# Part of an attention and MLP kernel's transfers moved from SyncE's queue to GpSimd's, and others held back

## The chip, the cores and the metric

The kernel runs on one core of a Trainium2 chip. The core has five engines that run side by side, each in its own order of instructions: TensorE (PE, with its weight loads shown apart as PEld), VectorE (DVE), ScalarE (ACT), GpSimd (POOL) and SyncE (SP). Data moves by DMA. An engine issues a transfer in its own instruction order (rows "SPq", "ACTq"), and 16 DMA engines carry it out; the issue takes a fraction of a microsecond, the landing several. The metric is the device time of one execution, in microseconds (us), the median of several runs.

## The reference

The kernel computes a gated mix of two branches over one sequence of 2048 tokens of 448 features, in float32. Cut to what matters:

```python
g = sigmoid((x * gate_w).sum(-1, keepdims=True))
q, k, v = split_heads(x @ wqkv)            # 16 heads of 28
idx = pos[:, None] - 2 * arange(8)         # 8 keys, every second position back
logits = einsum("bhsd,bhswd->bhsw", q, k[idx]) * 28 ** -0.5   # masked where idx < 0
a = einsum("bhsw,bhswd->bhsd", softmax(logits), v[idx]) @ wo
r = relu(x @ w1 + b1)                      # 1792 wide
b = (r * r) @ w2 + b2
out = g * a + (1 - g) * b
```

## The kernel before

Every float32 product is made of three matmuls of a shortened type: each operand is split into a high part (a ScalarE copy that rounds) and a low part (VectorE, or at one place GpSimd, subtracts the high part from the raw value), and high x high, high x low and low x high are added up in PSUM. So every weight and every token tile that arrives as a raw load costs ScalarE and VectorE an operation per slice before TensorE can use it. The contraction's last 64 rows are kept twice, so two matmuls of 64 rows run side by side on the two halves of TensorE; "a pair" or "a step" below is such a couple. When an accumulator changes halves, a one-element ScalarE instruction (`turn`, L360; `touch`, L748, in the MLP) orders the two halves. TensorE waits for these small instructions, and they stand in ScalarE's order with everything else.

Tokens come in four chunks of 512, chunk 0 to 3. Stage one makes q, k and v of each chunk (L353, L441): chunk 0 all at once (`qkv_first`), the others in two halves of two 128-token tiles (`qkv_two`). ScalarE evacuates the sums to staging tiles `st` (L375), of which there are three, and SP stores them to DRAM (`q_d`, `k_d`, `v_d`, L390). The last half of chunk 3 is woven with the first MLP matmuls. Then the MLP runs over the chunks in the order 3, 0, 1, 2. Token chunks are brought by `x_load` into one of two raw buffers and by `x_bring` into their split tiles (L727 on ScalarE, L730 on VectorE). Chunk 2 overwrites the tiles of chunk 0, and chunk 3 those of chunk 1, so the split tokens of chunks 0, 1 and 2 are first spilled to DRAM (`x_d`; L884 for chunk 0, `x_spill` L744 for 1 and 2) and reloaded for the MLP. w1 comes in four pieces (`w1_piece`: L675 into `early`, L665 into a raw buffer), the first half of w2 in two (`w2_piece`, L665; high parts L708, low parts L710), the second half row by row later.

Attention is not made on TensorE. It goes over eight units, two halves of the tokens (`par`) times four groups of four heads. For each unit, q and k (L513, L517) and v (L527) are loaded back from DRAM with eight tokens to a partition; GpSimd multiplies (`qk_piece` L551, `av_piece` L563), VectorE reduces (L555, L573), and a small softmax goes over GpSimd (mask L600, subtract the maximum L606, normalise L615), VectorE and ScalarE (exponent L607). The first unit can start when chunk 1's stores have landed. Its results go through DRAM and a transposing load to the output projection on TensorE (accumulators `a`), which is placed between MLP groups once its loads are in.

The order of all this on ScalarE, VectorE, GpSimd and SP is not written by hand. `Plan` is a list scheduler that runs while the program is built: each job has an engine, a cost, dependencies, a priority (TURN first, LAST last) and an earliest time `at`, in nanoseconds of the plan's own clock. A transfer is a job with `move=(packets, size)`; `wire` is the plan's time at which the DMA is free. `LAND` is an extra distance that a job keeps from a transfer it depends on, by the job's priority. When TensorE's order advances, `Plan.step` takes the jobs that can begin. On the chip only the order that results counts, with the semaphores: an engine executes its next instruction as soon as that one's operands are ready, and holds everything behind it until then.

All transfers but three small ones were issued by SP before the change.

Of the kernel before, what the change touches and what calls it, by code (L numbers as in the profile page):

```python
# [45 lines left out]
LAND = (0.0, 0.0, 500.0, 700.0, 2000.0, 2000.0)  # L46
# [10 lines left out]
class Plan:  # L57
# [4 lines left out]
    def __init__(self):  # L62
# [3 lines left out]
        self.port = self.wire = 0.0  # L66
# [29 lines left out]
    def begin(self, j):  # L96
        r = max(j.at, self.free[j.eng])
        for d in j.deps:
            e = self.end(d)
            if e is None:  # L100
                return None
            r = max(r, e + LAT + (LAND[j.prio] if d.eng == SYNC else 0.0))
        if j.prio > NEXT and r < self.hold[j.eng] < r + j.cost:
            r = self.hold[j.eng]
        if j.move and j.prio >= MID:
            r = max(r, self.wire - BACKLOG)
            if self.quiet[0] < r + j.cost < self.quiet[1]:
                r = self.quiet[1]
        if j.move and j.prio > NEXT:
            if r < self.calm < max(r + j.cost + 1250.0, self.wire) + j.move[0] * (8.0 + j.move[1] / 25.2) / 16 - 1250.0:  # L110
                r = self.calm
        return max(r, self.port) if j.port else r

    def step(self, limit):
# [70 lines left out]
def gated_mix_kernel(ctx: ExitStack, tc: tile.TileContext, xT, wqkv, w1, w2, wo, b1, b2, out):  # L185
# [87 lines left out]
    def dma(fn, packets, size, *deps, prio=MID, at=0.0):  # L273
        return add(SYNC, 430.0, fn, *deps, prio=prio, at=at, move=(packets, size))
# [216 lines left out]
    def attention():  # L491
# [130 lines left out]
        load_qk(1, *early_read)  # L622
        load_v(0)
# [21 lines left out]
    def gates(par):  # L645
        e = smp.tile([P, 32], F32, tag="e", name=f"e{par}")[:, :NS]
        a = add(ACT, 195.0, lambda: nc.scalar.activation(e, zt[:, par], AF.Exp, scale=-1.0), *z_jobs[par], prio=MID)
        a = add(ACT, 210.0, lambda: nc.scalar.activation(e, e, AF.Copy, bias=1.0), a, prio=MID)
        a = add(DVE, 200.0, lambda: nc.vector.reciprocal(gt[:, par], e), a, prio=MID)
        a = add(ACT, 195.0, lambda: nc.scalar.activation(g1t[:, par], gt[:, par], AF.Copy, scale=-1.0, bias=1.0), a)  # L650
        gate_jobs[par] = a
# [7 lines left out]
    def raw_load(i, name, src, view, packets, size, *deps, prio=MID, at=0.0):  # L659
# [3 lines left out]
        def load():  # L663
            hold[0] = rawp.tile([P, 4, 512], F32, tag="raw", name=name)
            nc.sync.dma_start(view(hold[0]), src)  # L665
        return hold, dma(load, packets, size, *held, *deps, prio=prio, at=at)
# [716 lines left out]
```

## Time and profile before

| | us |
|---|---|
| median of 3 runs | 392.4 |
| lowest and highest run | 392.34 and 511.83 |
| the profiled execution, its own time | 393.65 |
| its span, first to last instruction | 391.9 |

The granted TensorE clock was 0.998 of full speed. The span holds 9284 instructions and 73.76 MB of transfers. To read the rows: a timeline row has its start in us from the span's start, the duration of the merged instructions, engine, line, operation, output<-input by the program's names, the count (x), and in brackets how long the engine stood idle before it and what ended that. A row of a window has the window, its length, the busy time and count of PE, PEld, DVE, ACT and POOL, the granted clock, the mean busy share of the 16 DMA engines and GB/s. A row of the list of transfers has the size and the median time from issue to landing. In a wait row stand the total, the number of waits and the longest one.

### The profile page before, as it was taken

The numbers are of one execution on the slowest core, as the hardware profiler recorded it, in microseconds if no ns is written. First come the engines' busy times: TensorE is split into PE (matmuls) and PEld (weight loads), VectorE is DVE, ScalarE is ACT, GpSimd is POOL, SyncE is SP. The second block draws the span as 40 slices with busy tenths as digits, with TensorE's granted clock in tenths as the row PEclk, the third lists the DMA queues.
The fourth block names the chain that finished last, engine by engine and source line by source line (L and its number), as shares of the span: only waits on it lengthen the run. The fifth ranks groups of instructions, "written<-read, shape, count | busy, mean of one in ns | idle before, by whom it ended". The sixth has DMA issues, their size and how long they took to land.

```text
span 391.9 us, 9284 instructions
## 1 busy us (share of the span) xinstructions
PE 386.9 (99%) x3828; PEld 370.9 (95%) x3828; DVE 258.8 (66%) x348; ACT 205.8 (53%) x501; POOL 262.4 (67%) x171
## 2 busy tenths in 40 slices
PE   9999999999999999999999999999999999999996
PEld 8999999989999999999999999999999999999995
DVE  4525522477585778778655989779666686668454
ACT  4857866352566576444555545345616344456740
POOL 0000000999999999959999796999998979662000
PEclk9999999999999999999999999999999999999999
DMA  7999998998165062645203689655635220226745
GB/s 239 383 358 320 372 365 306 374 375 294 50 214 189 0 214 84 220 155 177 89 2 135 227 204 282 210 129 137 198 128 163 87 95 2 89 62 160 139 113 190
DMA packets 64955, 73.76 MB, mean 188 GB/s; under 512 B 32592, under 2 KB 57744, under 8 KB 64528
## 3 DMA queue, kind: packets, MB, share of 16 engines
q1 hardware_dynamic: 64480, 72.79, 57.5%
q8 instruction: 30, 0.49, 0.5%
q10 hardware_dynamic: 432, 0.38, 0.3%
q14 instruction: 13, 0.11, 0.1%
HBM read 45.71 MB, written 28.25 MB: 189 GB/s over the span
## 4 chain that ended last, share of the span: by engine, by line
PE 95%; DMA 3%; ACT 1%; SPq 0%; issue 0%; DVE 0%; DVEq 0%
PE b L353 32%; PE h L353 32%; PE qkv L353 19%; PE a L353 7%; DMA w2raw<-w 3%; PE qkv L441 2%; PE warm L819 1%; PE a L1173 1%; ACT w2ah L708 1%; SPq L390 0%; ACT qkv L360 0%; DVE bt_b L1056 0%; DVEq L1378 0%; SPq L665 0%
## 5 line engine op out<-in xcount | busy, mean ns | idle before, releaser
L551 POOL TENSOR_TENSOR pp<-q,k 128x896 f32<-128x896 f32 x56 | 116.6, 2120 | 77.9 <-DMA k<-k_d 66.9
L563 POOL TENSOR_TENSOR pp<-lg,v 128x896 f32<-128x896 f32 x64 | 113.9, 1870 | 9.6 <-DVE o L573 5.3
L353 PE MATMUL h<-x,w1h 64*128 64x512 f32 x672 | 109.9, 376 | 0.0
L353 PE MATMUL qkv<-wqh,x 64*128 64x448 f32 (+1 forms) x528 | 81.9, 350 | 0.7 <-ACT qkv L360 0.7
L555 DVE TENSOR_REDUCE lg<-pp 128x32 f32<-128x896 f32 x64 | 67.2, 1079 | 17.8 <-POOL pp L551 17.8
L805 DVE TENSOR_TENSOR h<-h,h 128x512 fp32r<-128x512 f32 x56 | 38.7, 691 | 50.8 <-ACT h L804 50.6
L353 PEld LDWEIGHTS h<-x,w1h 64*128 64x128 f32 x672 | 64.5, 186 | 7.6 <-DMA x<-x_d 0.3
L573 DVE TENSOR_REDUCE o<-pp 128x112 f32<-128x896 f32 x64 | 67.5, 1066 | 0.4 <-POOL pp L563 0.4
L353 PE MATMUL b<-w2bh,h 64*128 64x448 f32 x448 | 64.3, 349 | 0.0
L353 PE MATMUL b<-w2ah,h 64*128 64x448 f32 x448 | 64.2, 349 | 0.0
L353 PE MATMUL h<-x,w1l 64*128 64x512 f32 x336 | 64.2, 376 | 0.0
L353 PEld LDWEIGHTS qkv<-wqh,x 64*128 64x128 f32 x528 | 56.4, 186 | 1.0 <-ACT qkv L360 1.0
L801 ACT ACTIVATE h<-h,b1z 128x512 f32<-128x512 f32 x56 | 36.7, 655 | 37.0 <-PE h L353 37.0
L353 PE MATMUL qkv<-wql,x 64*128 64x448 f32 (+1 forms) x264 | 52.6, 349 | 0.0
L353 PEld LDWEIGHTS b<-w2ah,h 64*128 64x128 f32 x448 | 43.7, 193 | 0.7
L353 PEld LDWEIGHTS b<-w2bh,h 64*128 64x128 f32 x448 | 43.6, 193 | 0.7
L353 PE MATMUL b<-w2al,h 64*128 64x448 f32 x224 | 39.7, 349 | 0.0
L353 PE MATMUL b<-w2bl,h 64*128 64x448 f32 x224 | 39.7, 349 | 0.0
L353 PEld LDWEIGHTS h<-x,w1l 64*128 64x128 f32 x336 | 32.2, 186 | 3.3
L803 ACT ACTIVATE h<-h 128x512 fp32r<-128x512 f32 x56 | 33.4, 597 | 1.6
L375 ACT ACTIVATE st<-qkv 128x448 f32<-128x448 f32 x48 | 24.7, 540 | 16.6 <-PE qkv L353 9.0
L804 ACT ACTIVATE h<-h 128x512 f32<-128x512 f32 x56 | 33.2, 592 | 0.0
(111 smaller groups left out, 523.5 us busy)
## 6 DMA issues: line engine op xcount, KB each, us to landing
v<-v_d SPq DMA_DIRECT2D x8, 840.0 KB, 6.2
x_d<-x SPq DMA_DIRECT2D x12, 512.0 KB, 8.3
x<-x_d SPq DMA_DIRECT2D x12, 512.0 KB, 3.9
k<-k_d SPq DMA_DIRECT2D x7, 840.0 KB, 7.2
q_d<-st SPq DMA_DIRECT2D x8, 448.0 KB, 7.1
k_d<-st SPq DMA_DIRECT2D x8, 448.0 KB, 7.9
v_d<-st SPq DMA_DIRECT2D x8, 448.0 KB, 7.9
o_d<-o SPq DMA_DIRECT2D x16, 224.0 KB, 2.1
```

Source lines behind the costliest of these rows:

```text
L353: nc.tensor.matmul(woven_out(acc.pt, acc.n), a[rows], woven(w[rows]), start=acc.todo == acc.all, stop=acc.todo == 1)
L375: nc.scalar.activation(st[0][:, :, t % 2].rearrange("p (i g) c -> p i g c", i=2), unwoven(pt[:, :D]).rearrange("p i (g c) -> p i g c", c=C ...
L441: nc.tensor.matmul(woven_out(acc.pt, NQ), a, woven(w), start=k == j == 0, stop=False)
L551: nc.gpsimd.tensor_mul(pr.rearrange("p (w c) -> p w c", w=W), q[:, s:s + 1].to_broadcast([P, W, C]), k[:, s:s + W])
L555: nc.vector.tensor_reduce(lgs[i][:, s], pr.rearrange("p (w h d) -> p w h d", w=W, h=HG), axis=AX.X, op=ALU.add)
L563: nc.gpsimd.tensor_mul(pr.rearrange("p (h d w) -> p w h d", h=HG, w=W), lgs[i][:, s][:, :, :, None].to_broadcast([P, W, HG, DH]), vs[i][:, ...
L573: nc.vector.tensor_reduce(o_t[par, s][:, g * C:(g + 1) * C], pr.rearrange("p (c w) -> p c w", w=W), axis=AX.X, op=ALU.add)
L708: his = [add(ACT, cost_act(D), lambda k=k: nc.scalar.activation(w2ah[:, i0 + k], hold[0][:, k, :D], AF.Copy), got, prio=LATE) for k in ran ...
L801: a = add(ACT, 656.0, lambda pt=pt, r=r: nc.scalar.activation(pt, pt, AF.Relu, bias=b1t[:, f + r:f + r + 1]), ready, *bias_job[:2], prio=NEXT)
L803: b = add(ACT, 600.0, lambda pt=pt, hh=hh: nc.scalar.activation(hh, pt, AF.Square), a, prio=NEXT)
L804: a = add(ACT, 600.0, lambda pt=pt: nc.scalar.activation(pt, pt, AF.Square), b, prio=NEXT)
L805: low = add(DVE, 690.0, lambda pt=pt, hh=hh, hl=hl: nc.vector.tensor_sub(hl, pt, f32(hh)), a, prio=NEXT)
```

## The change

Fifteen transfers are issued by GpSimd instead of SP: the three token loads (chunks 1 to 3), the four w1 pieces, and the eight spills of chunks 0 and 1. The loads of w2's first half get an earliest planned time of 82000, the spill of chunk 2 one of 86000, the first unit's v one of 75000. The second unit's q and k depend on the landing of the first unit's. The gates of both token halves are made at once after chunk 3 instead of once after chunk 1 and once after chunk 3. The low parts of v's weights are made by one subtraction over three slices. The planner gets a wire for each of the two queues, an issue cost of 1000 on GpSimd, and a larger distance (`LAND`) for jobs of priority LATE, which the w1 and w2 copies have.

```diff
-LAND = (0.0, 0.0, 500.0, 700.0, 2000.0, 2000.0)
+W2_LOAD, X_SPILL, V_LOAD = 82000.0, 86000.0, 75000.0
+LAND = (0.0, 0.0, 500.0, 700.0, 4500.0, 2000.0)
...
-            self.free[SYNC] = s + j.cost + 45.0
-            self.wire = max(s + j.cost + 1250.0, self.wire) + packets * (8.0 + size / 25.2) / 16
-            j.done = self.wire + 450.0
+            self.free[j.eng] = s + j.cost + 45.0
+            other = POOL if j.eng == SYNC else SYNC
+            begin = max(s + j.cost + 1250.0, self.wire[j.eng])
+            time = packets * (8.0 + size / 25.2) / 16
+            both = min(time, max(0.0, self.wire[other] - begin) / 2)
+            self.wire[j.eng] = begin + time + both
+            self.wire[other] += both
+            j.done = self.wire[j.eng] + 450.0
...
-    def dma(fn, packets, size, *deps, prio=MID, at=0.0):
-        return add(SYNC, 430.0, fn, *deps, prio=prio, at=at, move=(packets, size))
+    queue = {SYNC: nc.sync, POOL: nc.gpsimd}
+
+    def dma(fn, packets, size, *deps, prio=MID, at=0.0, by=SYNC):
+        return add(by, 430.0 if by == SYNC else 1000.0, fn, *deps, prio=prio, at=at, move=(packets, size))
...
-        load_qk(1, *early_read)
-        load_v(0)
+        load_qk(1, *early_read, got["q", 0], got["k", 0])
+        load_v(0, event(V_LOAD))
...
-    def gates(par):
+    def gates():
...
-    def raw_load(i, name, src, view, packets, size, *deps, prio=MID, at=0.0):
+    def raw_load(i, name, src, view, packets, size, *deps, prio=MID, at=0.0, by=POOL):
...
-            nc.sync.dma_start(view(hold[0]), src)
-        return hold, dma(load, packets, size, *held, *deps, prio=prio, at=at)
+            queue[by].dma_start(view(hold[0]), src)
+        return hold, dma(load, packets, size, *held, *deps, prio=prio, at=at, by=by)
...
-            got = dma(lambda: nc.sync.dma_start(hold[0], w1[i]), 512, 1792, *deps, prio=MID)
+            got = dma(lambda: nc.gpsimd.dma_start(hold[0], w1[i]), 512, 1792, *deps, prio=MID, by=POOL)
...
-        hold, got = raw_load(buf, f"w2raw{i0}", w2[:, i0:i0 + n], lambda r: r[:, :n, :D], 128 * n, 1792, *deps, prio=MID)
+        hold, got = raw_load(buf, f"w2raw{i0}", w2[:, i0:i0 + n], lambda r: r[:, :n, :D], 128 * n, 1792, *deps, prio=MID, by=SYNC,
+                             at=W2_LOAD)
...
-        x_stored[c] = [dma(lambda j=j: nc.sync.dma_start(x_d[c, j], f32(x.t[j])), 128, 4096, *x.parts[j], prio=MID if c < 2 else LATE)
-                       for j in range(4)]
+        by = POOL if c < 2 else SYNC
+        x_stored[c] = [dma(lambda j=j: queue[by].dma_start(x_d[c, j], f32(x.t[j])), 128, 4096, *x.parts[j],
+                           prio=MID if c < 2 else LATE, by=by, at=0.0 if c < 2 else X_SPILL) for j in range(4)]
...
+    def wv_split():
+        n = block(2)
+        his = [add(ACT, cost_act(D), lambda k=k: nc.scalar.activation(wqh[:, k, n], raws[2][:, k], AF.Copy), event(13000.0),
+                   prio=SOON) for k in range(3)]
+        low = add(DVE, cost_dve(3 * D), lambda: nc.vector.tensor_sub(wql[:, :, n], raws[2], f32(wqh[:, :, n])), *his,
+                  prio=SOON, port=True)
+        for k in range(3):
+            wq_jobs[2, k] = (his[k], low)
...
-            gates(par)
+        if c == 3:
+            gates()
```

The order of instructions that the planner makes of it changes at three places that matter below. The first is ScalarE in chunk 3's first half, the place of w2's copies (`w2ah`). Before, they stand after the last evacuations of chunk 2 (`st`) and ahead of the first turns of chunk 3 (L360, accumulators `qkv_0_0` and so on, named by tile and kind: 0 is q, 1 is k, 2 is v):

```order
L375 ACTIVATE st_3_1_1179<-qkv_2_1_1049 128x4x112
L375 ACTIVATE st_2_2_1201<-qkv_3_2_1052 128x4x112
L708 ACTIVATE w2ah<-w2raw_1116 128x448 x4
L708 ACTIVATE w2ah<-w2raw_1155 128x448 x3
L360 ACTIVATE qkv_0_0_1222<-b1z 1x1
L360 ACTIVATE qkv_1_1_1225<-b1z 1x1
L360 ACTIVATE qkv_1_0_1223<-b1z 1x1
```

In the changed kernel (where L360 has become L369, L375 L384, L607 L616 and L708 L718) they stand after the last evacuations of chunk 3's first half, ahead of and between the turns of its second half, with the first unit's exponent (`lg`) among them:

```order
L384 ACTIVATE st_1_1_1360<-qkv_0_1_1225 128x4x112
L384 ACTIVATE st_0_2_1381<-qkv_1_2_1228 128x4x112
L718 ACTIVATE w2ah<-w2raw_1270 128x448 x4
L616 ACTIVATE lg_1015<-lg_1015 128x256
L369 ACTIVATE qkv_2_0_1403<-b1z 1x1
L369 ACTIVATE qkv_3_1_1406<-b1z 1x1
L718 ACTIVATE w2ah<-w2raw_1344 128x448
L369 ACTIVATE qkv_3_0_1404<-b1z 1x1
L369 ACTIVATE qkv_2_2_1407<-b1z 1x1
L718 ACTIVATE w2ah<-w2raw_1344 128x448 x2
```

Seven copies have moved half a chunk later, and the exponent, which stood after those turns, stands ahead of them. The second place is ScalarE at the start of chunk 1, where chunk 2's tokens are brought. Before, the four copies (`x_0` to `x_3` from `xraw`) lie among the turns:

```order
L360 ACTIVATE qkv_0_0_494<-b1z 1x1
L360 ACTIVATE qkv_1_1_497<-b1z 1x1
L727 ACTIVATE x_0_584<-xraw_244 128x512
L360 ACTIVATE qkv_1_0_495<-b1z 1x1
L360 ACTIVATE qkv_0_2_500<-b1z 1x1
L727 ACTIVATE x_1_585<-xraw_244 128x512
L727 ACTIVATE x_2_586<-xraw_244 128x512
L360 ACTIVATE qkv_0_1_496<-b1z 1x1
L360 ACTIVATE qkv_1_2_504<-b1z 1x1
L727 ACTIVATE x_3_587<-xraw_244 128x512
```

In the changed kernel (L727 is L737) all four lie ahead of the first turn:

```order
L737 ACTIVATE x_0_540<-xraw_257 128x512
L737 ACTIVATE x_1_541<-xraw_257 128x512
L737 ACTIVATE x_2_542<-xraw_257 128x512
L737 ACTIVATE x_3_543<-xraw_257 128x512
L369 ACTIVATE qkv_0_0_496<-b1z 1x1
L369 ACTIVATE qkv_1_1_499<-b1z 1x1
L369 ACTIVATE qkv_1_0_497<-b1z 1x1
```

So the turns now stand behind whatever those copies wait for. The third place is SP from the last stores of chunk 1 on. Before, the loads of the first and the second unit (`q`, `k` and `qk`) lie interleaved, and v and w2 follow:

```order
L390 DMA v_d<-st_2_2_842 128x4x224
L513 DMA q_931<-q_d 128x896
L513 DMA qk_939<-q_d 128x896
L517 DMA k_954<-k_d 128x1680
L517 DMA qk_939<-k_d 128x1680
L527 DMA v_976<-v_d 128x1680
L390 DMA q_d<-st_0_0_1001 128x4x224
L390 DMA k_d<-st_1_1_1011 128x4x224
L390 DMA v_d<-st_0_2_1029 128x4x224
L665 DMA w2raw_1116<-w 128x4x448
L665 DMA w2raw_1155<-w 128x3x448
```

In the changed kernel (L390 is L399, L513 L522, L517 L526) the second unit's come after the first unit's and the biases:

```order
L399 DMA v_d<-st_2_2_840 128x4x224
L522 DMA q_896<-q_d 128x896
L526 DMA k_926<-k_d 128x1680
L914 DMA b1z<-b 128x7
L915 DMA b1z<-b 128x7
L916 DMA b2t<-b 16x448 x2
L522 DMA qk_1012<-q_d 128x896
L526 DMA qk_1012<-k_d 128x1680
L399 DMA q_d<-st_0_0_993 128x4x224
```

The first unit's v and w2 now come later in the queue, w2's first load behind chunk 2's last stores, and w2's second behind the third unit's q and k. On GpSimd the moved transfers stand ahead of the first product, so that its order starts, after constants, with these:

```order
L674 DMA xraw_242<-xT 128x2048
L674 DMA xraw_257<-xT 128x2048
L684 DMA early<-w 128x1792
L905 DMA x_d<-x_0_177 128x1024
L905 DMA x_d<-x_1_178 128x1024
L905 DMA x_d<-x_2_179 128x1024
L905 DMA x_d<-x_3_180 128x1024
L684 DMA early<-w 128x1792
L674 DMA w1raw_557<-w 128x4x448
L755 DMA x_d<-x_353 128x1024 x4
L674 DMA xraw_665<-xT 128x2048
L674 DMA w1raw_787<-w 128x4x448
```

Before, none of these stood there; the first product followed the constants.

More of the change, by code (lines that the diff above doesn't have):

```diff
@@ L65, in __init__ @@
         self.jobs = {e: [] for e in self.free}
-        self.port = self.wire = 0.0
+        self.port = 0.0
+        self.wire = {SYNC: 0.0, POOL: 0.0}
         self.count = 0
@@ L101, in begin @@
                 return None
-            r = max(r, e + LAT + (LAND[j.prio] if d.eng == SYNC else 0.0))
+            r = max(r, e + LAT + (LAND[j.prio] if d.eng and d.move else 0.0))
         if j.prio > NEXT and r < self.hold[j.eng] < r + j.cost:
@@ L105, in begin @@
         if j.move and j.prio >= MID:
-            r = max(r, self.wire - BACKLOG)
+            r = max(r, self.wire[j.eng] - BACKLOG)
             if self.quiet[0] < r + j.cost < self.quiet[1]:
@@ L109, in begin @@
         if j.move and j.prio > NEXT:
-            if r < self.calm < max(r + j.cost + 1250.0, self.wire) + j.move[0] * (8.0 + j.move[1] / 25.2) / 16 - 1250.0:
+            if r < self.calm < max(r + j.cost + 1250.0, self.wire[j.eng]) + j.move[0] * (8.0 + j.move[1] / 25.2) / 16 - 1250.0:
                 r = self.calm
@@ L860, in gated_mix_kernel @@
     nc.vector.tensor_sub(x.x8, rx[:, 3], f32(x.x7))
-    plan.t, plan.wire = START, 15000.0
+    plan.t = START
+    plan.wire[SYNC] = 15000.0
     plan.now = 9800.0
```

24 lines of the change are left out of this document (12 added, 12 removed).

## The prediction

> **What bounds the kernel now.** I read the page first (busy shares, then the chain by engine), then TensorE's waits, then the timeline of TensorE at the one wait found there.
>
> ```profile
> PE 386.9 (99%) x3828; PEld 370.9 (95%) x3828; DVE 258.8 (66%) x348; ACT 205.8 (53%) x501; POOL 262.4 (67%) x171
> ...
> PE 95%; DMA 3%; ACT 1%; SPq 0%; issue 0%; DVE 0%; DVEq 0%
> ...
> PE qkv L353 <- ACT qkv L360: 0.7, 1, 0.7
> ...
> 83.24 0.35 PE L353 MATMUL qkv<-w7h,x 64*128 64x448 f32 x1
> 83.29 0.35 PE L353 MATMUL qkv<-wqh,x 64*128 64x448 f32 x1
> 84.31 0.46 PE L353 MATMUL qkv<-wqh,x 64*128 64x448 f32 x2 [0.67 <-ACT qkv L360]
> ```
>
> TensorE is busy in 386.9 of 391.9 us, and between its first matmul and its last one it waits once. Pairs start 0.19 us apart (82.87, 83.06, 83.24 in this stretch), so the next was due at 83.48 and came at 84.31: 0.83 us lost, of which the wait list counts 0.67. The chain's 3% "DMA" is the work behind that wait and not 3% of idle TensorE. Who held the wait, in the timelines of SP and ScalarE, a 10 us window and the list of transfers:
>
> ```profile
> 69.53 3.50 SPq L665 DMA_DIRECT2D w2raw<-w  x2
> ...
> 77.48 0.98 ACT L375 ACTIVATE st<-qkv 128x448 f32<-128x448 f32 x2
> 80.73 3.38 ACT L708 ACTIVATE w2ah<-w2raw 128x448 fp32r<-128x448 f32 x7 [2.27 <-DMA w2raw<-w]
> 84.02 0.61 ACT L360 ACTIVATE qkv<-b1z 1x1 f32<-1x1 f32 x6
> ...
> 70.00:80.00 10.00, 10.00 (x108) 10.00 (x107) 5.43 (x5) 3.63 (x12) 10.00 (x6) 1.00 1.06 376
> ...
> w2raw<-w SPq DMA_DIRECT2D x1, 896.0 KB, 11.2
> ```
>
> ScalarE had nothing else from 78.46 on, stood 2.27 us for w2's first load, which took 11.2 us on a full DMA (share 1.06), then copied seven slices for 3.38 us. The turns (L360), for which TensorE waits, stand behind them.
>
> **The change, part by part.**
> *w2 held back.* In the new order the seven copies leave this place for one half a chunk later; the turns then follow the evacuations that end at 78.46 and are done well before 83.48. Gain: 0.83 us, no more, since TensorE starts its pairs without a gap on both sides. What is late next is the place the copies go to (timelines of GpSimd, ScalarE, TensorE, VectorE):
>
> ```profile
> 68.33 16.52 POOL L551 TENSOR_TENSOR pp<-q,k 128x896 f32<-128x896 f32 x8 [66.89 <-DMA k<-k_d]
> 84.76 9.38 POOL L551 TENSOR_TENSOR pp<-qk 128x896 f32<-128x896 f32 x3
> 94.10 0.65 POOL L600 TENSOR_TENSOR lg<-lg,mask 128x256 f32<-128x256 f32 x1
> ...
> 98.81 0.64 POOL L606 TENSOR_TENSOR lg<-lg,mx 128x256 f32<-128x256 f32 x1
> ...
> 90.36 0.98 ACT L375 ACTIVATE st<-qkv 128x448 f32<-128x448 f32 x2 [0.72 <-PE qkv L353]
> ...
> 99.48 0.42 ACT L607 ACTIVATE lg<-lg 128x256 f32<-128x256 f32 x1 [0.17 <-POOL lg L606]
> ...
> 96.54 0.35 PE L353 MATMUL qkv<-wql,x 64*128 64x450 f32 x2
> ...
> 82.74 3.99 DVE L710 TENSOR_TENSOR w2al<-w2raw,w2ah 128x1792 fp32r<-128x1792 f32 x1 [0.89 <-ACT w2ah L708]
> ```
>
> There ScalarE now has, between the evacuations and the next turns, four w2 copies (3.38/7 = 0.48 each, 1.9 in all) and the first unit's exponent. Less the 0.83, the evacuations end at 90.5 and the copies at 92.4. TensorE first needs those turns where q's second half begins, one step ahead of the row at 96.54: 96.35, now 95.5. Turn pair 0.26 and exponent 0.42 leave 94.8 as the latest end of GpSimd's subtraction (L606). Ahead of that stand 13 products at 16.52/8 = 2.065, the mask 0.65 and the subtraction 0.64: 28.1 us. (Before it took 31.1: three products took 9.38 beside the w2 subtraction of 3.99 on VectorE, which now comes later.) So attention must start by 94.8 - 28.1 = 66.7 instead of 68.33.
>
> *Second unit's loads behind the first's.* The second unit's q (448 KB) no longer stands ahead of the first unit's k on SP:
>
> ```profile
> 59.28 0.33 SPq L513 DMA_DIRECT2D q<-q_d  x1
> 59.66 0.42 SPq L513 DMA_DIRECT2D qk<-q_d  x1
> 60.69 0.32 SPq L517 DMA_DIRECT2D k<-k_d  x1
> ...
> 58.00:60.00 2.00, 2.00 (x26) 2.00 (x24) 0.44 (x2) 1.52 (x6) 0.00 (x0) 1.00 0.76 237
> 60.00:62.00 2.00, 2.00 (x24) 2.00 (x22) 1.69 (x2) 1.88 (x10) 0.00 (x0) 1.00 0.89 299
> 62.00:64.00 2.00, 2.00 (x26) 2.00 (x24) 0.86 (x3) 1.67 (x5) 0.00 (x0) 1.00 0.95 341
> ```
>
> The windows' last two columns are the DMA's busy share and GB/s. 448 KB, 0.459 MB, at 341 GB/s is 1.3 us. With fifteen transfers on a queue of their own, the idle share of 58 to 62 can be filled too: 2 x 0.24 + 2 x 0.11 = 0.7 us. Start then at 68.33 - 2.0 = 66.3, 0.4 ahead of the limit: TensorE loses 0. Ends: no move at all, 68.33, costs 1.6 us of TensorE; the second unit's k (840 KB) out of the way too, 3.9 + 0.7, gives 63.7 and costs 0. I stand nearer the late end, because only one transfer's place is certain. The first values' load (held back) stood behind k already: 0.
>
> [...]
>
> *Fifteen transfers issued by GpSimd.* No row shows a DMA issue on GpSimd. The nearest are SP's issues of the same tiles (spills L744 and L884, token and w1 loads), then chunk 1 on ScalarE and TensorE:
>
> ```profile
> L744 SPq DMA_DIRECT2D x_d<-x x8: 426/704/3340, 34.3 to 83.1; - x8
> ...
> 10.70 0.93 SPq L665 DMA_DIRECT2D xraw<-xT  x2
> ...
> 23.82 3.40 SPq L884 DMA_DIRECT2D x_d<-x  x3
> ...
> DMA to landing us min/median/max: 6.4/7.6/7.6
> ...
> xraw<-xT SPq DMA_DIRECT2D x3, 1024.0 KB, 7.6
> early<-w SPq DMA_DIRECT2D x2, 896.0 KB, 8.8
> ...
> 20.00:30.00 10.00, 10.00 (x108) 10.00 (x108) 1.72 (x3) 5.25 (x16) 0.00 (x0) 1.00 0.99 351
> ...
> 34.22 0.26 ACT L360 ACTIVATE qkv<-b1z 1x1 f32<-1x1 f32 x2 [0.98 <-PE qkv L353]
> ...
> 36.37 0.63 ACT L727 ACTIVATE x<-xraw 128x512 fp32r<-128x512 f32 x1 [0.18 <-DVE x L730]
> ...
> 35.89 0.37 PE L353 MATMUL qkv<-wql,x 64*128 64x450 f32 x2
> ```
>
> Issue: 15 x 0.43 = 6 us to 15 x 3.34 = 50 us of GpSimd, between 10.7 and the 66.3 to which it waits for k anyway: 0 on the path. SP loses fifteen issues, none of which held TensorE: 0. What can cost is the landing. The four copies that bring chunk 2's tokens (L727) now stand ahead of chunk 1's first turns; they overwrite chunk 0's tokens, so they wait for its four spills (L884). TensorE needs the turns one step ahead of the row at 35.89, at 35.7; less a turn pair (0.26) and the last copy (0.63), the fourth spill must land by 34.8. By bytes: two token loads (1024 KB), a w1 piece (896), four spills (512) and SP's four stores beside them (448) are 6.95 MB, 19.8 us at 351 GB/s; from a first issue at 10.7 + 1 that is 31.5, 3.3 early, and TensorE loses 0. Other end: were each GpSimd transfer to land before the next moves, 11.7 + 2 x 7.6 + 8.8 + 4 x 7.6 = 66.1, a stall of 31.3. The first is nearer: SP issued three spills in 3.40 us though each took 7.6 to land, so transfers overlap.
>
> *The rest.* w2's second load (672 KB) stands on SP behind the third unit's q and k, which wait for the first unit's products, 66.3 + 16.5 = 82.8. With the issues it goes out at about 84 and, taking the 11.2 of the first again, lands by 95.2; its first copy is due ahead of the second turns, needed nine steps (1.7 us) after the first ones' 95.5: 95.2 + 0.48 + 0.26 = 95.9 of 97.2, so 0. Behind the same wait on SP stand the third spill, which nothing in this stretch reads, and the stores of chunk 3's first half, whose evacuations end only at 90.5: 0.
>
> ```profile
> 13.94 1.70 DVE L270 TENSOR_TENSOR wql<-wqraw,wqh 128x448 fp32r<-128x448 f32 x3 [0.98 <-ACT wqh L267]
> ...
> 60.30 1.56 DVE L682 TENSOR_TENSOR w1l<-w1raw,w1h 128x1344 fp32r<-128x1344 f32 x1 [1.86 <-ACT w1h L680]
> ...
> 23.22 0.35 PE L353 MATMUL qkv<-w7h,x 64*128 64x448 f32 x2
> ...
> 58.48 0.21 ACT L650 ACTIVATE zg<-zg 128x8 f32<-128x8 f32 x1 [1.02 <-DVE zg L649]
> ```
>
> V's low parts in one subtraction take 1.56 instead of 1.70; started after the third copy (14.8) they are there at 16.4, and the V matmuls begin nine steps ahead of the row at 23.22, at 21.5: 0. The gates at once drop one set of four small operations, which ended at 58.7 with nobody waiting: 0. TensorE's matmuls are the same 3828; a block of 42 of the output projection moves one group later: 0.
>
> Sum: the profiled execution took 393.65 (span 391.9 and 1.75 around it); less 0.83 it is 392.8. The median of the runs, 392.4, lies 1.25 below it; the same step gives **391.6**.
>
> **Rivals.**
> 1. *No room on the wire.* The bytes taken out of k's way are all: start 67.0, the exponent holds the turns 0.3 us, 391.9. For it: the shares near 1. Against: 0.76 and 0.89 just where k waits. [...]
> 2. *Attention hardly starts earlier*, since k also waits for its own stores. Each microsecond past 66.7 costs one; at 68.33 it is 393.2, slower than before. It decides against the change from a start of 67.5, where the 0.83 is used up. For it: SP issued k at 60.69, 1.0 after the second unit's q, so a wait stood between. Against: FIFO order on SP takes the 448 KB out.
> 3. *GpSimd's queue is slow* and the spills land late ahead of chunk 1's turns. Past 34.8 it costs one for one: break-even at 35.6, over 2% (8 us) past 43.4, and 423 at the serial end; at 37 to 38 it is 393.8 to 394.8. For it: no row shows this queue. Against: 3.3 us of room.
> 4. *The wait only moves*: w2's second load lands after 96.5 and holds the second turns; two microseconds late is 393.6. For it: 11.2 for the first on a full DMA. Against: it is smaller, and 1.57 MB of w2 have left the stretch ahead.
>
> **How the numbers follow.** Forecast 0.60, rival 1 0.14, rival 2 0.10, rival 3 0.11 (0.04 of it past 2%), rival 4 0.05. The forecast's own spread is about half a microsecond, that of its term: 391.0 to 392.1. From 391.0 to 394.0 lie the forecast, rivals 1, 2 and 4 and the mildest of 3. Two per cent is 7.8 us, about what a measurement of this kernel can tell from no change: faster by that 0.01 (the only wait is 0.83), slower 0.04, within it 0.95.
>
> **What would show it.** Right: no wait for L360 on TensorE, w2's copies after 90, first product at 65.5 to 66.7, GpSimd's last transfer issued before 55. Wrong: a TensorE wait near 35 (rival 3), or near 95 behind the exponent (1, 2) or behind a w2 copy (4).

## The result, and the profile after

The changed kernel takes 404.51 us (median of 6 runs, 402.85 to 406.16) against 392.44 before; the ratio is 1.0296 with an interval of 1.0276 to 1.0316. It is 3% slower where 391.6 (391.0 to 394.0) was forecast. The profiled execution took 403.14, span 401.3, against 393.65 and 391.9. So the two profiles differ by 9.5 us and the medians by 12.1: the profile of before lies 1.2 above its median and that of the change 1.4 below. The granted clock was 0.996 in the three faster runs of the change and 0.992 to 0.994 in the three slower ones; no trace shows what those three waited for.

First the page and the waits of TensorE after the change:

```profile
PE 390.3 (97%) x3828; PEld 371.5 (93%) x3828; DVE 260.6 (65%) x345; ACT 204.6 (51%) x498; POOL 270.8 (67%) x186
...
PE qkv L362 <- ACT qkv L369: 5.2, 2, 3.3
PE qkv L362 <- ACT st L384: 1.2, 2, 0.8
```

The one wait of before (0.7 behind w2's copies) is gone. In its place stand four others, 6.4 us together (and one of 0.3 for a reload near 310 us). The timeline of TensorE says where they are, and the windows (busy us and instructions of TensorE, of its weight loads, VectorE, ScalarE, GpSimd, then granted clock, DMA share, GB/s) what happened around them:

```profile
30.04 0.46 PE L362 MATMUL qkv<-wqh,x 64*128 64x448 f32 x2 [3.35 <-ACT qkv L369]
36.33 0.45 PE L362 MATMUL qkv<-wqh,x 64*128 64x448 f32 x1 [0.75 <-ACT st L384]
41.05 0.45 PE L362 MATMUL qkv<-wqh,x 64*128 64x448 f32 x1 [0.46 <-ACT st L384]
45.45 0.46 PE L362 MATMUL qkv<-wqh,x 64*128 64x448 f32 x2 [1.87 <-ACT qkv L369]
...
30.00:32.00 2.00, 1.96 (x14) 1.83 (x16) 0.00 (x0) 0.17 (x2) 0.54 (x1) 0.63 1.04 397
32.00:34.00 2.00, 2.00 (x14) 1.83 (x12) 0.00 (x0) 0.00 (x0) 0.54 (x1) 0.51 1.04 398
34.00:36.00 2.00, 1.58 (x17) 1.23 (x13) 0.00 (x0) 0.27 (x1) 0.45 (x1) 1.00 1.04 389
```

All of it lies between 26 and 46 us, in the chunks 0 and 1, far from the place that the change was meant for. After the wait of 3.35 us the granted clock was 0.63 and 0.51, and TensorE got 14 matmuls into 2 us where the undisturbed kernel gets 108 into 10; from 34 on it was 1.00 again.

The start of TensorE's n-th matmul, compared between two traces, turns this into a sum. The table gives for each execution how much later (+) or earlier it started the n-th matmul than the profiled execution of before:

| matmul | start before | changed kernel | fifteen on SP | all but the queue | w2 alone | before, second profile |
|---|---|---|---|---|---|---|
| 150 | 21.52 | +0.47 | +0.01 | +0.16 | -0.12 | -0.14 |
| 300 | 35.70 | +9.75 | +0.44 | +0.16 | -0.12 | -0.14 |
| 750 | 78.33 | +9.85 | +0.55 | +0.16 | -0.12 | -0.14 |
| 900 | 93.51 | +8.88 | -0.43 | -0.82 | -1.10 | -0.60 |
| 1200 | 123.57 | +8.89 | -0.42 | -0.63 | -0.66 | +0.67 |
| 3000 | 304.08 | +8.71 | -0.60 | -0.81 | -0.62 | +0.50 |
| 3150 | 319.30 | +9.45 | -0.23 | -0.16 | +0.03 | +0.49 |
| last | 388.02 | +9.45 | -0.23 | +0.02 | +0.21 | +0.50 |

(The other columns are experiments told below.) In the changed kernel 0.46 is there from the first microseconds; the four gaps add 3.52, 1.09, 0.79 and 2.06; the stretch at the low clock adds 1.8. That is 9.7 of the 9.85 that stand at matmul 750. Between matmuls 750 and 900 it then gains 0.97, the w2 wait that was removed, and between 3000 and 3150 it loses 0.74 to a wait for the reload of the last tokens.

Who held the four waits, in the timelines of ScalarE, SP and GpSimd, and SP's stores from issue to landing between 14 and 33 us:

```profile
21.17 0.52 ACT L384 ACTIVATE st<-qkv 128x448 f32<-128x448 f32 x1
28.45 1.42 ACT L384 ACTIVATE st<-qkv 128x448 f32<-128x448 f32 x3 [6.77 <-DMA q_d<-st]
...
35.73 0.54 ACT L384 ACTIVATE st<-qkv 128x448 f32<-128x448 f32 x1 [5.57 <-DMA q_d<-st]
...
40.45 0.54 ACT L384 ACTIVATE st<-qkv 128x448 f32<-128x448 f32 x1 [2.81 <-DMA k_d<-st]
...
16.74 1.61 SPq L399 DMA_DIRECT2D q_d<-st  x2
29.46 0.91 SPq L399 DMA_DIRECT2D k_d<-st  x2
...
10.53 1.27 POOL L674 DMA_DIRECT2D xraw<-xT  x2 [9.08 <-DMA wqraw<-wqkv]
11.78 0.53 POOL L684 DMA_DIRECT2D early<-w  x1
12.30 2.12 POOL L905 DMA_DIRECT2D x_d<-x  x4
18.03 0.55 POOL L684 DMA_DIRECT2D early<-w  x1 [3.60 <-DMA xraw<-xT]
27.18 0.77 POOL L674 DMA_DIRECT2D w1raw<-w  x1 [8.61 <-issue]
...
DMA to landing us min/median/max: 10.9/12.3/17.6
```

Read it from the end. ScalarE copies two finished blocks of q, k or v into a staging tile, and SP stores the tile; there are three. The fourth tile to be filled needs the first store to have landed. Before, these stores landed in 5.5 to 6.3 us (same view of the kernel before, 14 to 33 us: 5.5/6.1/6.3), so the tile was free in time. Now SP issues the first two from 16.74 on, much as it did (16.28 before), but they take 11.6 and 17.6. ScalarE stands 6.77 us at 28.45, and behind it in its order stand the turns (L369) for which TensorE waits. GpSimd, with nothing else to do and no wait on those transfers, had issued seven of them by 14.42 (two token loads, a w1 piece and four spills, 4992 KB or 5.1 MB); before, SP issued only the two token loads ahead of the q stores, and the spills after the k stores, at 23.82.

The list of queues from 22 to 26 us shows how the two then share the DMA:

```profile
DMA packets 714, 1.64 MB, mean 409 GB/s; under 512 B 39, under 2 KB 396, under 8 KB 714
...
q0 software_dynamic: 357, 1.32, 80.7%
q1 hardware_dynamic: 357, 0.32, 22.9%
```

q0 is GpSimd's queue, q1 SP's; the columns are packets, MB and share of the 16 engines' time. 357 against 357 packets: in these 4 us each queue got as many packets as the other, and since SP's stores move 896 bytes in one and GpSimd's mostly 4096 (its spills), the stores got a fifth of the bytes (0.32 of 1.64 MB). How the next packet is chosen the trace doesn't show.

### The profile page after: what moved, and what is told of

It is laid out like the page before. It is cut to its first block, busy times and chain, and to the rows that moved or that the text cites. A ratio compares the mean times of both kernels' runs of the same rounds, so it can differ in the third digit from the quotient of the medians.

```text
span 401.3 us, 9297 instructions
## 1 busy us (share of the span) xinstructions
PE 390.3 (97%) x3828; PEld 371.5 (93%) x3828; DVE 260.6 (65%) x345; ACT 204.6 (51%) x498; POOL 270.8 (67%) x186
## 3 DMA queue, kind: packets, MB, share of 16 engines
q0 software_dynamic: 2256, 11.01, 7.2%
## 4 chain that ended last, share of the span: by engine, by line
PE 86%; DMA 2%; ACT 0%; DVE 0%; DVEq 0%; issue 0%
PE h L362 31%; PE b L362 31%; PE qkv L362 16%; PE a L362 7%; DMA x<-x_d 2%; PE a L1195 1%; ACT x L737 0%; DVE bt_b L1078 0%; DVEq L1400 0%; ACT qkv L369 0%
## 5 line engine op out<-in xcount | busy, mean ns | idle before, releaser
L572 POOL TENSOR_TENSOR pp<-lg,v 128x896 f32<-128x896 f32 x64 | 117.0, 1907 | 12.7 <-DVE lg L564 9.8
L362 PE MATMUL qkv<-wqh,x 64*128 64x448 f32 (+1 forms) x528 | 82.8, 356 | 6.4 <-ACT qkv L369 5.2
L362 PEld LDWEIGHTS qkv<-wqh,x 64*128 64x128 f32 x528 | 57.3, 189 | 8.1 <-ACT qkv L369 5.9
L384 ACT ACTIVATE st<-qkv 128x448 f32<-128x448 f32 x48 | 24.3, 540 | 32.8 <-DMA q_d<-st 12.3
```

Source lines behind the costliest of these rows:

```text
L362: nc.tensor.matmul(woven_out(acc.pt, acc.n), a[rows], woven(w[rows]), start=acc.todo == acc.all, stop=acc.todo == 1)
L384: nc.scalar.activation(st[0][:, :, t % 2].rearrange("p (i g) c -> p i g c", i=2), unwoven(pt[:, :D]).rearrange("p i (g c) -> p i g c", c=C ...
L572: nc.gpsimd.tensor_mul(pr.rearrange("p (h d w) -> p w h d", h=HG, w=W), lgs[i][:, s][:, :, :, None].to_broadcast([P, W, HG, DH]), vs[i][:, ...
```

## The experiments

Theory 1 was that this sharing by packets made the stores late; theory 2, that transfers issued by GpSimd are slow in themselves; theory 3, that only the order and the bytes ahead of the stores count, whoever issues them. Each kernel starts from the changed one unless it is said otherwise.

**The fifteen on SP**, everything else in the same order.

```diff
-    queue = {SYNC: nc.sync, POOL: nc.gpsimd}
+    queue = {SYNC: nc.sync, POOL: nc.sync}
...
-            got = dma(lambda: nc.gpsimd.dma_start(hold[0], w1[i]), 512, 1792, *deps, prio=MID, by=POOL)
+            got = dma(lambda: nc.sync.dma_start(hold[0], w1[i]), 512, 1792, *deps, prio=MID, by=POOL)
...
-    x_stored[0] = [dma(lambda j=j, x=x: nc.gpsimd.dma_start(x_d[0, j], f32(x.t[j])), 128, 4096, event(11500.0), prio=MID,
+    x_stored[0] = [dma(lambda j=j, x=x: nc.sync.dma_start(x_d[0, j], f32(x.t[j])), 128, 4096, event(11500.0), prio=MID,
```

> The fifteen transfers are issued by SP in place of GpSimd, every other instruction of every engine in the order of the changed kernel. Theory 1 (the DMA engines take packets from the two queues in turn, one for one, so SP's stores of 896 bytes each get a small share beside GpSimd's packets of 4096 to 8192 bytes; the three staging tiles come free late, ScalarE's evacuations wait, TensorE waits) and theory 2 (GpSimd's transfers are slow in themselves): no TensorE wait between 20 and 46 us, 391.3 to 392.3, the 0.83 us of w2 kept. Theory 3 (it is the order and the bytes ahead of the stores, whoever issues them): stores still late, 396 or more. If the cost lies in another part of the change (w2, the second unit's loads, the gates): 400 or more.

393.48 us (12 runs), ratio 1.002 (1.0006 to 1.0034). TensorE's only wait between 20 and 46 us is this:

```profile
36.14 0.46 PE L362 MATMUL qkv<-wqh,x 64*128 64x448 f32 x2 [0.24 <-ACT qkv L369]
```

So 11 of the 12 us come from GpSimd issuing the fifteen. The stores took 7.0 to 9.5 us here, and that was still early enough. The time is 1.2 above the expected upper end. The table's column shows 0.5 lost by matmul 750, 0.98 gained behind it, and 0.37 lost again near 310; but it ends 0.23 ahead of a profile of before that is itself slow, so it doesn't show why the median lies 0.65 above that of before.

**The fifteen on ScalarE's queue** (the same three lines with `nc.scalar`).

> The fifteen transfers are issued by ScalarE in place of GpSimd, order otherwise that of the changed kernel. Theory 1: any second queue beside SP's does it, so SP's stores land late again, the same waits for the staging tiles between 20 and 46 us, 399 to 406. Theory 2 (GpSimd's own transfers are slow): the stall is gone, 391.5 to 394. Theory 3: as theory 1. A ScalarE held up by its own issues would show as waits for the issue and not for the staging tiles.

395.49 (4 runs), ratio 1.0057 (1.004 to 1.0073). The profiled execution, 397.76, is the slowest of the four. In it the stall between 20 and 46 us is gone, which theory 1 in its simple form, that any second queue does it, did not allow. But ScalarE could issue the four spills only at 20.54, 23.87, 24.47 and 26.81, between its own instructions, and not at 12.3 to 14.4. Its loss comes later, where late v stores keep ScalarE waiting:

```profile
45.28 0.54 ACT L384 ACTIVATE st<-qkv 128x448 f32<-128x448 f32 x1 [3.06 <-DMA v_d<-st]
...
51.22 0.74 PE L362 MATMUL qkv<-wqh,x 64*128 64x448 f32 x2 [2.71 <-ACT qkv L369]
```

It leaves open whether the kind of the queue matters or the time of issue. The next ones ask that.

**Spills of 1024 bytes**: the spilled tokens' layout in device memory is cut so that a row of 4096 bytes becomes four pieces.

```diff
-    x_d = tc.dram_tile([3, 4, P, 2, CH], F32, name="x_d")
+    x_d = tc.dram_tile([3, 4, 2, 2, P, CH // 2], F32, name="x_d")
...
+    def x_rows(c, j):
+        return x_d[c, j].rearrange("i h p n -> p i h n")
```

> Only the layout of the spilled tokens in device memory is changed, so that each spill and reload moves packets of 1024 bytes in place of 4096; same queues, same bytes, same order. Theory 1: beside the spills the stores' share by bytes rises from 896/(896+4096) = 18% to 896/(896+1024) = 47%, the staging tiles come free earlier, the 6.4 us of TensorE's waits fall to 0 to 3 and the time to 392 to 398. Theory 2 and theory 3: same bytes ahead and same queue, 403 to 405, or later since there are four times as many packets.

410.27 (2 runs), ratio 1.0447 (1.0429 to 1.0465): a miss in every direction. GpSimd's timeline shows why it answers another question:

```profile
12.51 0.77 POOL L912 DMA_DIRECT2D x_d<-x  x1
26.50 0.78 POOL L912 DMA_DIRECT2D x_d<-x  x1 [13.21 <-issue]
30.23 0.75 POOL L912 DMA_DIRECT2D x_d<-x  x1 [2.95 <-issue]
36.05 0.76 POOL L912 DMA_DIRECT2D x_d<-x  x1 [5.07 <-issue]
```

After one spill of the finer kind GpSimd issued no other for 13.21 us; the tokens that wait for the fourth spill then came late. In the changed kernel a like wait came after eight transfers (8.61, until 27.18); VectorE had read the raw buffer that this transfer fills until 22.19, so 5.0 of it had no such reason. The spills' packets are still recorded with 4096 bytes (GpSimd's queue has 2256 packets and 11.01 MB in both kernels), so the share of the stores was not tested.

**Stores by SP and ScalarE in turn.**

```diff
+            eng = (nc.sync, nc.scalar)[len(stores[b, par]) % 2]
-            j = dma(lambda: nc.sync.dma_start(dd.rearrange("p g s c -> p g (s c)"),
+            j = dma(lambda: eng.dma_start(dd.rearrange("p g s c -> p g (s c)"),
```

> The stores of the staging tiles are issued by SP and ScalarE in turn in place of SP alone; the fifteen stay on GpSimd. Theory 1: the stores then hold two of three queues, 2 x 896 of 2 x 896 + 4096 bytes = 30% in place of 18%, so they land about 1.7 times as fast and the waits of 6.4 us fall to 2 to 4: 395 to 400. Theory 2 and theory 3: no change of the landing, 402 to 406.

405.77 (2 runs), ratio 1.0332 (1.0306 to 1.0359): no gain, against the expected 395 to 400. From 22 to 26 us the three queues carried

```profile
q0 software_dynamic: 299, 1.08, 66.4%
q1 hardware_dynamic: 301, 0.27, 19.3%
q10 hardware_dynamic: 292, 0.26, 18.7%
```

packets, nearly one for one for one. But each whole store still had one queue, which the expectation overlooked, and it is the first store that ScalarE waits for (until 28.70).

**Each store as two halves, one by SP and one by ScalarE.**

```diff
-            j = dma(lambda: nc.sync.dma_start(dd.rearrange("p g s c -> p g (s c)"),
-                                              st[0].rearrange("p g s c -> p g (s c)")), 512, 896, *st[2], prio=SOON)
+            def store():
+                to, fr = dd.rearrange("p g s c -> p g (s c)"), st[0].rearrange("p g s c -> p g (s c)")
+                nc.sync.dma_start(to[:, :G // 2], fr[:, :G // 2])
+                nc.scalar.dma_start(to[:, G // 2:], fr[:, G // 2:])
+
+            j = dma(store, 512, 896, *st[2], prio=SOON)
```

> The changed kernel, but each store of a staging tile is two transfers of half the size, one issued by SP and one by ScalarE, so each single store now has two queues beside GpSimd's (with whole stores issued by the two in turn, each store still had one and the first landed no sooner). Sharing packet for packet: the first store of 512 packets gets 2 of 3 turns, about 320 packets in 2 us in place of 170, so it lands near 24.5 in place of 28.4; TensorE's waits between 20 and 46 us fall from 6.4 to 0 to 3 us, the time to 393 to 399. If a newcomer only stands behind what was queued before it (first come, first served over all queues): no change, 402 to 406.

400.46 (2 runs), ratio 1.0195 (1.0169 to 1.0221). The same bytes, the same GpSimd queue, and ScalarE gets its tile 2.8 us sooner:

```profile
25.61 1.42 ACT L384 ACTIVATE st<-qkv 128x448 f32<-128x448 f32 x3 [4.42 <-DMA q_d<-st]
...
q0 software_dynamic: 302, 1.10, 67.6%
q10 hardware_dynamic: 303, 0.26, 18.7%
q1 hardware_dynamic: 302, 0.26, 18.6%
```

25.61 was expected near 24.5, and first come, first served would have left it at 28.4. This is the run that shows the sharing by packets at work in the time: 4.0 us less than the changed kernel. TensorE itself went on only 0.9 sooner (29.10 for 30.04), since ScalarE now spent 2.12 us issuing its halves of the k stores ahead of the turns. And the sharing is not the whole: TensorE still waits 4.4 us, and 400.46 lies above the expected 393 to 399.

**The fifteen on GpSimd, but paced**: behind each of chunk 0's stores GpSimd reads one number of the staging tile.

```diff
+            def store():
+                nc.sync.dma_start(dd.rearrange("p g s c -> p g (s c)"), st[0].rearrange("p g s c -> p g (s c)"))
+                if c == 0:
+                    nc.gpsimd.tensor_copy(tick[0:1, 0:1], st[0][0:1, 0, 1, 0:1])
```

> The fifteen stay on GpSimd, but behind each of chunk 0's six stores GpSimd reads one number of the staging tile, so it can issue a transfer only after the evacuations that stand ahead of it in the planned order (in the changed kernel it issued seven of them, 4.9 MB, by 14.4 us, since nothing held it). Theory A (the cost is the burst: transfers issued all at once ahead of SP's first store at 16.7, with which the stores then share the DMA engines packet for packet): first store lands by 22, no wait for a staging tile between 20 and 46, 391.5 to 394. Theory B (transfers of GpSimd's queue slow the stores whenever they are issued): waits for staging tiles remain, 399 to 405.

403.25 (4 runs), ratio 1.0252 (1.0225 to 1.028). By 27 us the wait was 0.98 in place of 3.35, but the loss came back later:

```profile
27.70 1.58 POOL L909 DMA_DIRECT2D x_d<-x  x3 [0.29 <-issue]
29.28 0.54 POOL L688 DMA_DIRECT2D early<-w  x1
...
30.90 2.16 SPq L400 DMA_DIRECT2D v_d<-st  x2
...
45.40 0.54 ACT L384 ACTIVATE st<-qkv 128x448 f32<-128x448 f32 x1 [4.99 <-DMA v_d<-st]
...
50.96 0.45 PE L362 MATMUL qkv<-wqh,x 64*128 64x448 f32 x1 [2.74 <-ACT zg L390]
56.31 0.46 PE L362 MATMUL qkv<-wqh,x 64*128 64x448 f32 x2 [2.81 <-ACT qkv L369]
```

Held back, the spills and the w1 pieces stand ahead of and beside the v stores instead of the q stores. So the early burst is one place of the loss and not the whole cause: theory A fell, and here GpSimd's transfers held up the v stores instead.

**The burst on SP's own queue**: the first w1 piece and chunk 0's spills issued by SP right behind the second token load, ahead of the q stores.

```diff
             queue[by].dma_start(view(hold[0]), src)
+            if name == "xraw2":
+                nc.sync.dma_start(early[:, 0], w1[1])
+                for j in range(4):
+                    nc.sync.dma_start(x_d[0, j], f32(xs[0].t[j]))
```

> As the kernel with the fifteen on SP, but the first w1 piece and chunk 0's four spills stand on SP ahead of the first q store: the same burst as GpSimd made, on SP's own queue and first in, first out. Theory A with sharing by packets: here the stores don't share, they come right behind 5.0 MB, so at 395 GB/s the first lands at about 10.4 + 12.7 + 1.2 + 1 = 25 and the second at 26.5, against 27.7 and 30 in the changed kernel; waits of TensorE 1 to 4 us, 393 to 399. If only the bytes ahead counted, whichever the queue: as the changed kernel, 401 to 406. If GpSimd's queue is the cause: 391.5 to 393.5.

399.22 (2 runs), ratio 1.0161 (1.0141 to 1.0182). No second queue is there, and yet

```profile
29.16 1.42 ACT L384 ACTIVATE st<-qkv 128x448 f32<-128x448 f32 x3 [7.99 <-DMA q_d<-st]
```

ScalarE gets its first tile back 4 us later than expected from the bytes ahead, and TensorE waits 4.6. So an order that puts the burst ahead of the stores costs some 6 us by itself, with no second queue; theory 2 is not needed for it. The other 5.3 of the changed kernel (404.51 against 399.22) belong to what GpSimd's queue did beyond that: its second q store landed 17.6 us after the issue, at 35.6, and here 12.9 after it, at 30.4. In the changed kernel GpSimd's transfers got as many packets as SP's stores (357 and 357 from 22 to 26 us), and GpSimd also issued two more w1 pieces and chunk 1's spills from 18.03 to 36.1; these two causes are not told apart.

**Half of the fifteen**: the eight spills back to SP with the loads on GpSimd, and the reverse (the `dma_start` of these lines on `nc.sync`).

> The eight spills of chunks 0 and 1 go back to SP, at their planned places between the stores; the three token and four w1 loads stay on GpSimd. Theory A: the burst is 3.0 MB in place of 4.9, ends near 19, and only the second w1 piece shares with the stores: no stall or one below 2 us, 391.5 to 395. Theory B: the loads alone still slow the stores, 396 to 404.

> The other half: the seven loads go back to SP at their planned places, the eight spills stay on GpSimd, which issues chunk 0's four at once near 12. Theory A: four spills (2.1 MB in 4096 byte packets) share with the token loads from 12 on and push everything back, the first store behind the tokens to about 23 to 25: waits of 1 to 5 us, 394 to 402. Theory B: 396 to 405. Neither: 391.5 to 393.

399.41 (2 runs; 1.0166, 1.0098 to 1.0234) and 398.85 (2 runs; 1.0152, 1.0132 to 1.0172). Each half alone costs about 6 us of the 12 (the two runs of the first lie 4.4 apart). The first was expected below 395: two token loads and two w1 pieces, all issued by 13.4 in packets of 8192 and 7168 bytes, are enough to keep ScalarE from its tile until 30.65. Sharing alone doesn't explain that. By the packet records, 980 of the 1024 packets of the two q stores had started by 27.0; SP's queue from 27 to 30 us then held

```profile
q1 hardware_dynamic: 37, 0.07, 5.9%
```

5.9% of 16 engines' time is about what one engine has (a sixteenth is 6.3%). So by this share, an estimate, the first store waited at the end for one or two DMA engines while the others were past it; the records don't name the engine, and what held the last packets is not shown. In the second half the spills, issued before the first weights had all landed, shared with the last weight loads from 12 to 18 us, 460 packets of GpSimd's against 479 of SP's, and TensorE waited behind those weights:

```profile
q0 software_dynamic: 460, 1.69, 69.0%
q1 hardware_dynamic: 479, 0.78, 34.0%
...
18.44 0.54 PE L362 MATMUL qkv<-wqh,x 64*128 64x448 f32 x2 [1.98 <-ACT qkv L369]
```

**All of the change but the queue**: the planner counts the fifteen as SP's and places them again.

```diff
-    def raw_load(i, name, src, view, packets, size, *deps, prio=MID, at=0.0, by=POOL):
+    def raw_load(i, name, src, view, packets, size, *deps, prio=MID, at=0.0, by=SYNC):
...
-        by = POOL if c < 2 else SYNC
+        by = SYNC
```

> All of the change but the queue: the planner itself counts the fifteen as SP's and places them as in the kernel before; w2, the first values and the third spill held back, the second unit's loads behind the first's, the gates at once. If the loss is GpSimd's queue alone and the gain is w2's 0.83 us: 391.6 to 392.2 and no TensorE wait of 0.5 us or more. If another part costs too: 393 or more.

**w2 held back alone**, put into the kernel before.

```diff
-LAND = (0.0, 0.0, 500.0, 700.0, 2000.0, 2000.0)
+LAND = (0.0, 0.0, 500.0, 700.0, 4500.0, 2000.0)
+W2_LOAD = 82000.0
...
-        hold, got = raw_load(buf, f"w2raw{i0}", w2[:, i0:i0 + n], lambda r: r[:, :n, :D], 128 * n, 1792, *deps, prio=MID)
+        hold, got = raw_load(buf, f"w2raw{i0}", w2[:, i0:i0 + n], lambda r: r[:, :n, :D], 128 * n, 1792, *deps, prio=MID,
+                             at=W2_LOAD)
```

> The kernel before with one part of the change: w2's two loads held back to the same place. The wait for w2's copies (0.83 us) goes; attention starts at 68.3 as before, later than the 66.7 that the prediction gave as the limit. By the prediction's rival 2 the exponent then holds the second turns of the last chunk: 392.8 to 393.5, no faster than before. If the limit was set too early: 391.6 to 392.2, and the second unit's loads add nothing.

393.78 (8 runs) and 393.91 (5 runs), both with ratio 1.0032 (1.0019 to 1.0045): a third of a per cent slower than before, not faster. Yet the wait is gone in both, and the exponent doesn't hold the turns. With w2 alone attention started early too (GpSimd's first product, ScalarE's exponent and the turns after it):

```profile
66.52 16.56 POOL L552 TENSOR_TENSOR pp<-q,k 128x896 f32<-128x896 f32 x8 [65.08 <-DMA k<-k_d]
...
94.63 0.42 ACT L608 ACTIVATE lg<-lg 128x256 f32<-128x256 f32 x1 [0.52 <-POOL lg L607]
95.50 0.26 ACT L361 ACTIVATE qkv<-b1z 1x1 f32<-1x1 f32 x2 [0.44 <-PE qkv L354]
```

That is 66.5 without the second unit's loads being moved (66.49 with them). In the two profiles of before it started at 68.33 and 69.77. So moving the second unit's loads added nothing that can be seen. Nor did w2's loads stand in k's way: before, SP issued them at 69.53, after the first product had begun. With w2 held back the planner also orders other transfers anew (three of chunk 1's spills, not two, ahead of chunk 1's first q store on SP); which of these moves brought k forward is not shown. By the table both stand about 1 us earlier at matmul 900 than before, and both have given it back at the end: 0.2 to 0.4 by 1200, and 0.65 near 310 us where before has no gap. That makes them level with a profile of before that lies about 1 us above its median; what else keeps their medians above that of before is not shown.

**The kernel before again**, unchanged.

> The kernel before once more, unchanged, for a second profiled execution: the first one took 393.65 us, more than any of its timed runs (392.34 to 393.36), and showed TensorE waiting 0.83 us for w2's copies. If that wait belongs to the kernel, it is there again, near 0.83, and removing it should have given 0.8 in the kernels with w2 held back. If it belongs to that execution (w2's first load took 11.2 us), this one shows 0 to 0.4 at that place and a span of 390.8 to 391.3, and there was nothing to gain: that would explain why the kernels with w2 held back are no faster.

392.7 (10 runs), ratio 0.9996 (0.9986 to 1.0005). Its profiled execution took 394.15, span 392.4, so the expected shorter span was a miss; its waits are

```profile
PE b L353 <- DVE h L805: 0.5, 1, 0.5
PE qkv L353 <- ACT qkv L360: 0.2, 1, 0.2
PE h L353 <- ACT w1h L748: 0.2, 1, 0.2
```

The wait behind w2's copies is 0.2 in place of 0.7 (by the starts of the matmuls 0.52 in place of 0.97 us lost), and others stand at places where the first trace had none. The wait that the prediction took off is there, but its size is not a constant of the kernel. Both profiled executions of before lie above its median; what such an execution of 392.4 waits for, no trace shows.

No kernel measured here beats the one before.

## Why the prediction was wrong, step by step

- **Fifteen transfers issued by GpSimd: the step that failed.** It said: "SP loses fifteen issues, none of which held TensorE: 0", and then looked for the cost in one place only, the landing of the four spills. That part came true: they were to land by 34.8 and were estimated at 31.5; issued from 12.3 to 13.9 they took 12.9 to 16.1 us, so the last was there by 30.0. What was left out are the transfers that stayed on SP. Its stores had a term in the bytes ("SP's four stores beside them") but none in time, so nobody asked when they would land and who waits for that. The trace of before held the chain: stores of 5.5 to 6.3 us, three staging tiles, evacuations ahead of the turns on ScalarE. With landings of 10.9 to 17.6 us it cost 9.3 (7.5 in four gaps, 1.8 at the low clock) in the profiled execution; in the medians it is 11 against the fifteen on SP.
- **Three things inside that step.** Issues on SP were not only a cost: SP's own waits spaced the transfers, and GpSimd, without a product until 73.55, had few. Issued by SP in one burst ahead of the stores, part of the fifteen cost 6 us too. Then, the sum went by bytes, as if a queue's share of the DMA were the bytes it brings; from 22 to 26 us, with work on both queues, they got as many packets each (357 and 357). Halving the stores over two queues gave ScalarE its tile 2.8 us sooner at the same bytes. And a mean rate hides the last packets: with the loads alone on GpSimd, 44 of 1024 were still to start 3.6 us before the first tile came free.
- **The rival that named the place** (GpSimd's queue slow, spills late, a wait near 35) had the right neighbourhood and the wrong mechanism. Its chance past 2% was 0.04. The waits begin at 26.5, not at 35, and behind stores, not spills.
- **w2 held back: -0.83.** The mechanism was right: no wait there, and TensorE gains 0.97 between matmuls 750 and 900. The size was an execution's, not the kernel's: a second trace of the same kernel loses 0.52 there, not 0.97, and the step took the wait off a median that lies 1.25 below the execution in which it was seen. Part of what was gained was lost later, 0.74 near 310 us in the changed kernel. So the sum of the other parts is not -0.83 but, with the fifteen placed on SP, +1.0 in the medians (393.78 against 392.78); why it is above zero stays open.
- **Attention must start by 66.7, estimated 66.3.** The time came out, 66.5 in the kernels with the fifteen on SP and with w2 alone, and the exponent held nothing. In the changed one attention starts at 73.55, with TensorE 9.85 later, and again the exponent holds nothing. The cause given (the second unit's q out of the way, and idle DMA time filled) was not needed: 66.52 came with those loads and the fifteen where they had been on SP. So this hit was luck as to its reason. w2's loads (1568 KB, which is 1.61 MB and not rival 4's 1.57) were not in k's way either.
- **w2's second load, values, third spill, v's low parts, gates: 0.** None shows a wait of TensorE after the change.
- **What the range missed.** 391.0 to 394.0 contains the kernels with the fifteen on SP in the planned order (393.48, 393.78) and the one with w2's part alone (393.91), and none that puts any of them on a second queue or, on SP, ahead of the stores.

## What to carry to other kernels

Before a transfer is moved to another queue, list what stays on the old one and who waits for it: here, from 22 to 26 us, the moved transfers took 80.7% of the 16 DMA engines' time beside 22.9% for those that stayed, at 357 packets each, so that packets of mostly 4096 bytes left those of 896 a fifth of the bytes (0.32 of 1.64 MB). GpSimd, with nothing else to do, issued seven transfers by 14.42; the waits of a busy issuer are a schedule, and moving the issues throws it away. A wait of less than a microsecond in one trace is to be looked up in a second one before it is counted as a gain.

## What the runs showed of the hardware that was not expected

- Issue on GpSimd was cheap: 0.53 us for a spill or a w1 piece into `early`, 0.77 for one into a raw buffer, 0.64 for a token load. It is the landing that was dear: 12.9 to 16.1 us for chunk 0's spills.
- GpSimd stood between its issues where the trace names nothing that it waited for: after eight transfers the next came 8.61 us later (5.0 after its buffer was free), and with finer pieces the second spill 13.21 after the first. What held it there is not shown.
- The length of a wait alone doesn't tell whether TensorE's granted clock falls. The paced kernel waited 2.74 us until 50.96 and the clock stayed at 1.00; after 2.81, until 56.31, it was 0.66 and then 0.50:

```profile
50.00:52.00 2.00, 1.04 (x10) 1.04 (x12) 0.07 (x1) 1.63 (x5) 0.00 (x0) 1.00 0.88 291
56.00:58.00 2.00, 1.69 (x10) 1.60 (x12) 1.91 (x5) 1.26 (x8) 0.00 (x0) 0.66 0.10 31
58.00:60.00 2.00, 2.00 (x14) 1.86 (x13) 0.12 (x1) 0.16 (x1) 0.77 (x1) 0.50 0.00 0
```

  With the fifteen on ScalarE's queue it fell after 2.71, less than the 2.74 that left it at 1.00 (0.76 from 50 to 52 us, 0.50 from 52 to 54), and with the spills alone on GpSimd after 1.98 (0.93 from 10 to 20 us, 0.90 from 20 to 30). In the changed kernel the low stretch lasted 3.41 us at 0.50, from 30.54 to 33.95, with 1.00 before and behind it. What decides between the cases is not shown.
- A store's last packets came long after most of the others: with the burst on SP's queue the first tile was given back at 29.16, and by 29.0 us 1000 of the 1024 packets of both q stores had started. The traces don't name the engine of a packet, so why the last 24 came late stays open. Whether a fourth staging tile would cover late stores was not tried.
